# Weight loading with separate result tiles, three landing buffers and shifts shared between two engines

## Chip, core and metric

The kernel runs on one core of one Trainium2 chip. The metric is the device time of one execution in microseconds (us); the kernel before was timed three times, and the median of those runs is the figure to compare with. One further execution was taken with the hardware profiler, and all rows of the profile below come from that one.

## The reference

The inputs are q, k and v of shape 8 x 8 x 576 x 64 (batch, heads, sequence, head size) and two weight matrices, `w_in` (512 x 2048) and `w_out` (2048 x 512), all float32 in meaning. The weights reach the kernel as 64-bit words, so each weight takes 8 bytes in memory.

```python
scores = q @ k.T / sqrt(64)
# heads 0..3: keys 0 <= query - key < 32; heads 4..7: key <= query, key % 32 == query % 32
attn   = softmax(where(mask, scores, -1e9))
x      = (attn @ v)            # regrouped to 4608 tokens x 512
h      = x @ w_in
out    = (h * cos(h)) @ w_out  # 4608 x 512, float32
```

## The kernel before

**Blocks and chunks.** The feed-forward part runs over 12 blocks `j` of 384 tokens, and in each over 16 chunks `f` of 128 hidden features. `hidden(j, f)` (L353 to L376) makes 12 matmuls into one of two PSUM banks named `h`: every product of float32 numbers is made of three products of a high and a low half (`wi_h`, `wi_l`, `x_hi`, `x_lo`). Then ScalarE rounds h / 2 pi (L364), VectorE reduces the argument (L365), ScalarE takes the sine (L368), VectorE multiplies with h (L371), ScalarE makes the high half `g_hi` (L374) and GpSimd the low half `g_lo` (L375). The bank is free again when L371 has read it. `outer(j, f)` adds nine matmuls (L382) with `wo_h` and `wo_l`; it runs three chunks behind `hidden` (`LAG = 3`).

**Stages.** First comes the attention of batches 0 and 1, with matmuls that only keep TensorE busy (L442). In it `load_x` (L341 to L352) brings blocks 0 and 1 from `xT`, a buffer in device memory to which attention writes its results. The second stage alternates chunks of blocks 0 and 1 while the weights arrive: the loop calls `need_weights(f)`, `chunk(0, f)`, `need_weights(f + 2)` and `chunk(1, f - 1)`. At its end it loads block 2. The third stage interleaves blocks 2 to 11 with the attention of batches 2 to 7.

**A weight load.** `load_weight` (L111 to L130) is called 32 times, for `w_in` and `w_out` of each of the 16 chunks. It takes one tile `raw` of 128 x 512 pairs of 32-bit words (512 KB) from the pool `cv`, which has two buffers, and fills it by one DMA from the queue of SyncE, SP (L114). The pairs are the low and the top words of float64 numbers. Five passes put the float32 together inside `raw` itself and split it: VectorE shifts the low words right by 29 (L116), VectorE adds the sign (L119), ScalarE scales the top words (L124), VectorE shifts and merges them in (L125), ScalarE makes the high half (L129), GpSimd subtracts to get the low half (L130). L130 reads the tile as well, so the buffer can be filled again only after L130.

**Order.** The program is laid out by a planner that simulates its time and puts each engine's instructions in one fixed order; on the chip every engine and every DMA queue runs its own list in that order, and an instruction that waits holds up all behind it. `order` adds an edge for the planner: L116 of chunk `f` comes no earlier than the VectorE step L365 of chunk `f - 2` of block 0. From block 2 on, `in_turn` fixes the order of the matmuls.

**x.** `load_x` lands each of the four 128 x 384 tiles of a block in a tile `x_raw` from its own pool with two buffers (L347); VectorE copies it to `x_hi` (L348) and GpSimd writes the difference to `x_lo` (L349). `x_hi` and `x_lo` have eight buffers each, so two blocks.

Of the kernel before, what the change touches and what calls it, by code (L numbers as in the profile page):

```python
# [12 lines left out]
F32 = mybir.dt.float32  # L13
F32R = mybir.dt.float32r
BF16 = mybir.dt.bfloat16
I32 = mybir.dt.int32
AF = mybir.ActivationFunctionType
ALU = mybir.AluOpType
AX = mybir.AxisListType
# [5 lines left out]
P = 128  # L25
# [18 lines left out]
TB = 384  # L44
# [24 lines left out]
def attention_cos_ffn(ctx, tc, qkl, vl, qkvs, w_in, w_out, eye, eye16, mask_l0, mask_l, mask_s, out):  # L69
    nc = tc.nc  # L70

    const = ctx.enter_context(tc.tile_pool(name="const", bufs=1))
# [1 line left out]
    ps_h = ctx.enter_context(tc.tile_pool(name="ps_h", bufs=2, space=bass.MemoryType.PSUM))  # L74
    ps_o = ctx.enter_context(tc.tile_pool(name="ps_o", bufs=1, space=bass.MemoryType.PSUM, reuse_waits="tile"))
    sm = ctx.enter_context(tc.tile_pool(name="sm", bufs=4))
    xp = ctx.enter_context(tc.tile_pool(name="xp", bufs=2))
    rp = ctx.enter_context(tc.tile_pool(name="rp", bufs=2))
    xs = ctx.enter_context(tc.tile_pool(name="xs", bufs=2 * NKC))

# [4 lines left out]
    ms = const.tile([P, GB], BF16, name="ms")  # L85
    for t, src in ((ident16, eye16), (ms, mask_s), (ident, eye), (ml0, mask_l0), (ml, mask_l)):
        nc.scalar.dma_start(out=t, in_=src)
    shift1, shift2, quarter = (const.tile([P, 1], F32, name=n) for n in ("shift1", "shift2", "quarter"))
    for t, value in ((shift1, -SHIFT), (shift2, -SHIFT - STEP), (quarter, math.pi / 2.0)):
        nc.vector.memset(t, value)  # L90
    warm = const.tile([P, 64], BF16, name="warm")
# [7 lines left out]
    def order(later, first, reason):  # L99
        tc.add_manual_dep(  # L100
            later.ins, first.ins.name,
            mybir.DependencyInfo(mybir.DependencyClass.NoSync, mybir.DependencyReason.DATA), reason=reason,
        )

    wi_h = const.tile([P, NFC, NKC, P], F32R, name="wi_h")
    wi_l = const.tile([P, NFC, NKC, P], F32R, name="wi_l")
    wo_h = const.tile([P, NFC, DM], F32R, name="wo_h")
    wo_l = const.tile([P, NFC, DM], F32R, name="wo_l")
    xT = dram.tile([P, NKC, NTOK], F32, name="xT")

    def load_weight(cv, src, hi, lo, after):  # L111

        raw = cv.tile([P, 512, 2], I32, name="raw")
        nc.sync.dma_start(out=raw.rearrange("p n w -> p (n w)"), in_=src)  # L114
        low, top = raw[:, :, 0], raw[:, :, 1]
        first = nc.vector.tensor_scalar(out=low, in0=low, scalar1=29, scalar2=None, op0=ALU.logical_shift_right)  # L116
        if after is not None:
            order(first, after, "weights no earlier than they are needed")
        nc.vector.scalar_tensor_tensor(  # L119
            out=low, in0=top, scalar=-0x80000000, in1=low, op0=ALU.bitwise_and, op1=ALU.bitwise_or  # L120
        )


        nc.scalar.activation(out=top.bitcast(F32), in_=top.bitcast(F32), func=AF.Copy, scale=2.0 ** -112)  # L124
        nc.vector.scalar_tensor_tensor(  # L125
            out=low, in0=top, scalar=3, in1=low, op0=ALU.logical_shift_left, op1=ALU.bitwise_or
        )
        w = low.bitcast(F32)
        nc.scalar.copy(out=hi, in_=w)  # L129
        nc.gpsimd.tensor_tensor(out=lo, in0=w, in1=hi.bitcast(F32), op=ALU.subtract)  # L130

    weights = 0

    def need_weights(cv, f):
        nonlocal weights
        for f in range(weights, f + 1):
            after = reduced[f - AHEAD] if 0 <= f - AHEAD < len(reduced) else None
            load_weight(
                cv, w_in.bitcast(I32)[f], wi_h[:, f].rearrange("p c n -> p (c n)"),
                wi_l[:, f].rearrange("p c n -> p (c n)"), after,  # L140
            )
            load_weight(cv, w_out.bitcast(I32)[f], wo_h[:, f], wo_l[:, f], after)
            weights = f + 1

    turn = None
# [9 lines left out]
    class Attention:  # L155
# [39 lines left out]
        def softmax(self, s, mask, n, w, pn=None):  # L195
# [15 lines left out]
            if self.plain:  # L211
                exps.append(nc.scalar.activation(out=e, in_=t, func=AF.Exp, scale=0.125))
            else:
                nc.scalar.activation(out=e, in_=t, func=AF.Silu, bias=shift1, scale=0.0625)  # L214
                nc.scalar.activation(out=t, in_=t, func=AF.Silu, bias=shift2, scale=0.0625)
                nc.vector.scalar_tensor_tensor(
                    out=e, in0=t, scalar=-math.exp(STEP), in1=e, op0=ALU.mult, op1=ALU.add
                )
                nc.scalar.activation(out=e, in_=e, func=AF.Square, scale=math.exp(SHIFT) / STEP)
            z = sm.tile([P, SU], F32, name="z")  # L220
# [120 lines left out]
    def load_x(j):  # L341
        his, los = [], []
        for c in range(NKC):
            raw = xp.tile([P, TB], F32, name="x_raw")
            hi = xs.tile([P, TB], F32R, name="x_hi")
            lo = xs.tile([P, TB], F32R, name="x_lo")
            nc.sync.dma_start(out=raw, in_=xT[:, c, j * TB:(j + 1) * TB])  # L347
            nc.vector.tensor_copy(out=hi, in_=raw)  # L348
            nc.gpsimd.tensor_tensor(out=lo, in0=raw, in1=hi.bitcast(F32), op=ALU.subtract)  # L349
            his.append(hi)  # L350
            los.append(lo)
        return his, los  # L352

    def hidden(j, f, x_hi, x_lo):
# [7 lines left out]
        r = rp.tile([P, TB], F32, name="r")  # L362
        k = r.bitcast(I32)
        nc.scalar.activation(out=k, in_=h, func=AF.Copy, scale=1.0 / (2.0 * math.pi), bias=0.25)  # L364
        red = nc.vector.scalar_tensor_tensor(out=r, in0=k, scalar=-2.0 * math.pi, in1=h, op0=ALU.mult, op1=ALU.add)  # L365
# [31 lines left out]
    def chunk(j, f, x, acc):  # L397
        pend.append((j, f, *hidden(j, f, *x), acc))
        if len(pend) > LAG:
            outer(*pend.pop(0))  # L400

    def accumulators(pool):
        return [pool.tile([P, DM], F32, name=f"acc{t}") for t in range(NTT)]

    def in_stages(units, knots, lag):


        begun = np.interp(range(len(units)), [n for _, n in knots], [at for at, _ in knots]).astype(int).tolist()
        steps = {}
        for n, (at, unit) in enumerate(zip(begun, units)):  # L410
            second = min([at + lag] + begun[n + 2:n + 3])
            for stage in (at, second, second + 1):
                steps.setdefault(stage, []).append(unit)
        return steps
# [9 lines left out]
    def step(steps, n):  # L424
        for unit in steps.get(n, ()):
            next(unit, None)

    with ExitStack() as loading:
        cv = loading.enter_context(tc.tile_pool(name="cv", bufs=2))
        with ExitStack() as stack:  # L430

            ps = stack.enter_context(tc.tile_pool(name="ps", bufs=1, space=bass.MemoryType.PSUM, reuse_waits="tile"))
            att = Attention(
                stack, True, ((ps_h, "h"), (ps_h, "h"), (ps, "acc0")), ((ps_o, "acc0"), (ps_o, "acc1")),
                ((ps_o, "acc2"), (ps, "acc3")), ld_bufs=3,
            )
            steps = in_stages(att.units(0) + att.units(1), ((0, 0), (20, 20)), 2)
            spare = ps.tile([P, 512], F32, name="acc2")

            def keep_busy(n, after):  # L440
                for _ in range(n):
                    mm = nc.tensor.matmul(  # L442
                        spare[:64], warm, warm.unsqueeze(1).broadcast_to([P, 8, 64]), start=True, stop=True
                    )
                    if after is not None:
                        order(mm, after, "in its place")
                    after = mm

            keep_busy(BUSY[0], None)
            for n in range(max(steps) + 1):  # L450
                step(steps, n)
                if n + 1 < len(BUSY):
                    keep_busy(BUSY[n + 1], att.scored)
                if n == LOADS[0]:
                    x0 = load_x(0)
                if n == LOADS[1]:
                    x1 = load_x(1)

        gp = ctx.enter_context(tc.tile_pool(name="gp", bufs=LAG + 1, side="right", reuse_waits="tile"))

        with ExitStack() as stack:
            op = stack.enter_context(tc.tile_pool(name="op", bufs=2, reuse_waits="tile"))
            ps_o1 = stack.enter_context(
                tc.tile_pool(name="ps_o1", bufs=1, space=bass.MemoryType.PSUM, reuse_waits="tile")
            )
            acc0, acc1 = accumulators(ps_o), accumulators(ps_o1)
            for f in range(NFC + 1):
                if f < NFC:
                    need_weights(cv, f)
                    chunk(0, f, x0, acc0)  # L470
                    need_weights(cv, min(f + AHEAD, NFC - 1))
                if f >= 1:
                    chunk(1, f - 1, x1, acc1)
            cur, acc = load_x(2), accumulators(ps_o)
            for f in range(LAG):
                chunk(2, f, cur, acc)


    with ExitStack() as stack:
# [6 lines left out]
        for n in range(LAG, (NTB - 2) * NFC):  # L486
            j, f = 2 + n // NFC, n % NFC
# [105 lines left out]
```

## Time and profile before

| what | value |
|---|---|
| runs | 1000.22, 1000.85, 1001.1 us; median 1000.85 |
| profiled execution | 999.46 us, of which the span of the core 997.7 us |
| mean granted TensorE clock | 0.995 |
| TensorE busy with matmuls | 968.3 us, 97% of the span |
| VectorE, ScalarE, GpSimd busy | 466.5, 499.2 and 385.2 us |
| bytes moved by DMA | 80.14 MB, of which 32 weight loads of 512 KB |

In the profile PE is TensorE, PEld its weight loads, DVE VectorE, ACT ScalarE, POOL GpSimd and SP SyncE; a q behind a name is the engine's DMA or instruction queue. A row of groups gives line, engine, operation, output and input tiles, the count, then busy time in us and the mean of one in ns, then the idle time before it and what ended it. A row of waits reads "who waited <- for what: us in total, times, longest us". A row of windows gives, for a stretch of the span, the busy time of each engine with its number of instructions, then the granted TensorE clock, the share of the DMA engines in use, and GB/s.

### The profile page before, as it was taken

To read this page: it belongs to the slowest core of one execution; us is meant where nothing else is said; L and a number is where in the kernel's file an instruction comes from. 1 tells how busy PE (TensorE), PEld (TensorE's weight loads), DVE (VectorE), ACT (ScalarE), POOL (GpSimd) and SP (SyncE) were. 2 spreads that over 40 slices of the span, in tenths; PEclk is the share of its full clock that TensorE was granted. 3 is DMA by queue.
4 is the path that set the end of the run, shared out by engine and by line. 5 is a ranking of instruction groups with operands and counts; after the bars stand their busy time and mean duration, and the time that the engine had idled before them with its cause. 6 is when DMAs were issued, how large, how long until landed. Compare 5 with 4: busy or idle time off the path is not lost.

```text
span 997.7 us, 17749 instructions
## 1 busy us (share of the span) xinstructions
PE 968.3 (97%) x6890; PEld 847.5 (85%) x6890; DVE 466.5 (47%) x1005; ACT 499.2 (50%) x1043; POOL 385.2 (39%) x418
## 2 busy tenths in 40 slices
PE   8988988998999999999999999999999999999998
PEld 5777877877888888888888888888888888889997
DVE  6866677655454444434344444444344444322222
ACT  3655555565555555455445545554454544433433
POOL 2555554544344344333333344434243333332221
PEclk9999999999899999999999999999999999999999
DMA  8963333232322222111211322211221310100000
GB/s 247 300 199 103 111 108 112 80 105 73 102 85 88 70 79 84 42 50 59 83 58 35 110 79 76 82 50 53 88 59 34 98 55 29 41 20 1 33 1 32
DMA packets 48228, 80.14 MB, mean 80 GB/s; under 512 B 5904, under 2 KB 33296, under 8 KB 48144
## 3 DMA queue, kind: packets, MB, share of 16 engines
q1 hardware_dynamic: 38208, 69.35, 23.1%
q10 hardware_dynamic: 9936, 9.65, 2.8%
q8 instruction: 54, 0.88, 0.4%
q14 instruction: 30, 0.25, 0.1%
HBM read 60.11 MB, written 18.87 MB: 79 GB/s over the span
## 4 chain that ended last, share of the span: by engine, by line
PE 78%; DMA 4%; DVE 2%; ACT 1%; issue 1%; POOL 0%; DVEq 0%; POOLq 0%; ACTq 0%; SPq 0%
PE h L358 35%; PE acc L382 34%; DMA raw<-in_w_out 2%; PE acc L249 2%; PE acc L265 2%; PE acc L316 2%; PE acc L290 2%; PE acc L257 1%; PE acc L302 1%; DVE raw L116 1%; DMA raw<-in_w_in 1%; DMA xT<-x_t 0%; ACT r L368 0%; DVE r L371 0%; DVE raw L119 0%
## 5 line engine op out<-in xcount | busy, mean ns | idle before, releaser
L375 POOL TENSOR_TENSOR g_lo<-r,g_hi 128x384 fp32r<-128x384 f32 x192 | 198.3, 1033 | 396.6 <-issue 249.2
L358 PE MATMUL h<-x_hi,wi_h 128*128 128x384 f32 x768 | 267.9, 349 | 13.7 <-DVE r L371 13.7
L358 PE MATMUL h<-x_hi,wi_l 128*128 128x384 f32 x768 | 259.7, 338 | 0.0
L358 PE MATMUL h<-x_lo,wi_h 128*128 128x384 f32 x768 | 259.4, 338 | 0.0
L365 DVE SCALAR_TENSOR_TENSOR r<-r,h 128x384 f32<-128x384 int32 x192 | 106.1, 552 | 270.8 <-ACT r L364 247.7
L382 PE MATMUL acc<-wo_l,g_hi 128*128 128x512 f32 x576 | 227.4, 395 | 0.0
L382 PE MATMUL acc<-wo_h,g_hi 128*128 128x512 f32 x576 | 224.2, 389 | 1.4 <-ACT g_hi L374 1.4
L382 PE MATMUL acc<-wo_h,g_lo 128*128 128x512 f32 x576 | 224.6, 396 | 0.0
L358 PEld LDWEIGHTS h<-x_hi,wi_h 128*128 128x128 f32 x768 | 145.2, 189 | 31.0 <-DVE r L371 19.8
L368 ACT ACTIVATE r<-r,quarter 128x384 f32<-128x384 f32 x192 | 118.5, 617 | 96.5 <-DVE r L365 96.2
L358 PEld LDWEIGHTS h<-x_lo,wi_h 128*128 128x128 f32 x768 | 145.3, 189 | 5.0
L371 DVE TENSOR_TENSOR r<-r,h 128x384 f32<-128x384 f32 x192 | 106.0, 552 | 84.0 <-ACT r L368 83.4
L358 PEld LDWEIGHTS h<-x_hi,wi_l 128*128 128x128 f32 x768 | 145.1, 189 | 0.1
L364 ACT ACTIVATE r<-h 128x384 int32<-128x384 f32 x192 | 93.4, 487 | 102.0 <-PE h L358 95.5
L374 ACT CAST g_hi<-r 128x384 fp32r<-128x384 f32 x192 | 98.3, 512 | 87.5 <-DVE r L371 87.2
L382 PEld LDWEIGHTS acc<-wo_h,g_lo 128*128 128x128 f32 x576 | 108.0, 188 | 22.8
L382 PEld LDWEIGHTS acc<-wo_h,g_hi 128*128 128x128 f32 x576 | 108.3, 188 | 19.0 <-ACT g_hi L374 1.7
L382 PEld LDWEIGHTS acc<-wo_l,g_hi 128*128 128x128 f32 x576 | 108.0, 187 | 18.2
L349 POOL TENSOR_TENSOR x_lo<-x_raw,x_hi 128x384 fp32r<-128x384 f32 x48 | 50.9, 1062 | 130.9 <-DVE x_hi L348 107.4
L214 ACT ACTIVATE e_sb<-t_sb,shift 128x288 f32<-128x288 f32 (+1 forms) x60 | 32.9, 548 | 95.6 <-POOL t_sb L206 95.6
L348 DVE CAST x_hi<-x_raw 128x384 fp32r<-128x384 f32 x48 | 21.6, 452 | 60.9 <-DMA x_raw<-xT 60.2
L206 POOL TENSOR_TENSOR t_sb<-t_sb,mx 128x288 f32<-128x288 f32 (+1 forms) x60 | 41.6, 693 | 16.9 <-DVE mx L205 11.5
(66 smaller groups left out, 855.8 us busy)
## 6 DMA issues: line engine op xcount, KB each, us to landing
qk<-in_qkvs SPq DMA_DIRECT2D x32, 324.0 KB, 3.7
qk<-in_qkl SPq DMA_DIRECT2D x48, 208.0 KB, 3.3
x_raw<-xT SPq DMA_DIRECT2D x48, 192.0 KB, 2.4
out<-o SPq DMA_DIRECT2D x36, 256.0 KB, 2.1
raw<-in_w_in SPq DMA_DIRECT2D x16, 512.0 KB, 3.7
raw<-in_w_out SPq DMA_DIRECT2D x16, 512.0 KB, 3.8
v<-in_vl SPq DMA_DIRECT2D x48, 144.0 KB, 2.2
xT<-x_t ACTq DMA_DIRECT2D x16, 288.0 KB, 3.5
```

Of the source, the lines that this page charges most:

```text
L206: nc.gpsimd.tensor_tensor(out=t, in0=t, in1=mx[:, :n].unsqueeze(2).broadcast_to([P, n, w]), op=ALU.subtract)
L214: nc.scalar.activation(out=e, in_=t, func=AF.Silu, bias=shift1, scale=0.0625)
L348: nc.vector.tensor_copy(out=hi, in_=raw)
L349: nc.gpsimd.tensor_tensor(out=lo, in0=raw, in1=hi.bitcast(F32), op=ALU.subtract)
L358: mm = nc.tensor.matmul(h, w[:, f, c], x[c], start=(i == 0), stop=(i == len(ops) - 1))
L364: nc.scalar.activation(out=k, in_=h, func=AF.Copy, scale=1.0 / (2.0 * math.pi), bias=0.25)
L365: red = nc.vector.scalar_tensor_tensor(out=r, in0=k, scalar=-2.0 * math.pi, in1=h, op0=ALU.mult, op1=ALU.add)
L368: sin = nc.scalar.activation(out=r, in_=r, func=AF.Sin, bias=quarter)
L371: nc.vector.tensor_tensor(out=r, in0=r, in1=h, op=ALU.mult)
L374: nc.scalar.copy(out=g_hi, in_=r)
L375: nc.gpsimd.tensor_tensor(out=g_lo, in0=r, in1=g_hi.bitcast(F32), op=ALU.subtract)
L382: mm = nc.tensor.matmul(acc[t], g[:, ts], w[:, f], start=(f == 0 and i == 0), stop=(f == NFC - 1 and i == 2))
```

## The change

The kernel after differs in three places. In `load_weight` the float32 is put together in a tile of its own, `bits` (128 x 512, two buffers), and `raw` has three buffers; what reads `raw` last is then L125 of the kernel before. For `w_out` the first shift is done by a ScalarE activation that reads the low word as an unsigned integer, multiplies, adds a bias and rounds to an integer; for `w_in` it stays on VectorE. The ordering edge is kept for the VectorE shift only. In `load_x` the DMA lands in the tile of the low half, and GpSimd subtracts in place; the pool of `x_raw` is gone. Three small constants share one tile.

```diff
-    xp = ctx.enter_context(tc.tile_pool(name="xp", bufs=2))
...
-    shift1, shift2, quarter = (const.tile([P, 1], F32, name=n) for n in ("shift1", "shift2", "quarter"))
+    biases = const.tile([P, 3], F32, name="biases")
+    shift1, shift2, quarter = (biases[:, n:n + 1] for n in range(3))
...
-    def load_weight(cv, src, hi, lo, after):
+    def load_weight(cv, src, hi, lo, after, scalar):
...
-        first = nc.vector.tensor_scalar(out=low, in0=low, scalar1=29, scalar2=None, op0=ALU.logical_shift_right)
-        if after is not None:
-            order(first, after, "weights no earlier than they are needed")
+        bits, scaled = cv.tile([P, 512], I32, name="bits", bufs=2), top.bitcast(F32)
+        if scalar:
+            nc.scalar.activation(
+                out=bits, in_=low.bitcast(U32), func=AF.Copy, scale=2.0 ** -29 * (1.0 - 2.0 ** -16),
+                bias=7.5 * 2.0 ** -16 - 0.5,
+            )
+        else:
+            first = nc.vector.tensor_scalar(out=bits, in0=low, scalar1=29, scalar2=None, op0=ALU.logical_shift_right)
+            if after is not None:
+                order(first, after, "weights no earlier than they are needed")
         nc.vector.scalar_tensor_tensor(
-            out=low, in0=top, scalar=-0x80000000, in1=low, op0=ALU.bitwise_and, op1=ALU.bitwise_or
+            out=bits, in0=top, scalar=-0x80000000, in1=bits, op0=ALU.bitwise_and, op1=ALU.bitwise_or
         )
...
         nc.vector.scalar_tensor_tensor(
-            out=low, in0=top, scalar=3, in1=low, op0=ALU.logical_shift_left, op1=ALU.bitwise_or
+            out=bits, in0=top, scalar=3, in1=bits, op0=ALU.logical_shift_left, op1=ALU.bitwise_or
         )
-        w = low.bitcast(F32)
+        w = bits.bitcast(F32)
...
-                wi_l[:, f].rearrange("p c n -> p (c n)"), after,
+                wi_l[:, f].rearrange("p c n -> p (c n)"), after, False,
...
-            load_weight(cv, w_out.bitcast(I32)[f], wo_h[:, f], wo_l[:, f], after)
+            load_weight(cv, w_out.bitcast(I32)[f], wo_h[:, f], wo_l[:, f], after, True)
...
-            raw = xp.tile([P, TB], F32, name="x_raw")
             hi = xs.tile([P, TB], F32R, name="x_hi")
             lo = xs.tile([P, TB], F32R, name="x_lo")
+            raw = lo.bitcast(F32)
...
-        cv = loading.enter_context(tc.tile_pool(name="cv", bufs=2))
+        cv = loading.enter_context(tc.tile_pool(name="cv", bufs=3))
```

More of the change, by code (lines that the diff above doesn't have):

```diff
@@ L16 @@
 I32 = mybir.dt.int32
+U32 = mybir.dt.uint32
 AF = mybir.ActivationFunctionType
@@ L115, in load_weight @@
         low, top = raw[:, :, 0], raw[:, :, 1]
-        first = nc.vector.tensor_scalar(out=low, in0=low, scalar1=29, scalar2=None, op0=ALU.logical_shift_right)
-        if after is not None:
-            order(first, after, "weights no earlier than they are needed")
+        bits, scaled = cv.tile([P, 512], I32, name="bits", bufs=2), top.bitcast(F32)
[8 more added lines that the diff above has]
+                order(first, after, "weights no earlier than they are needed")
         nc.vector.scalar_tensor_tensor(
-            out=low, in0=top, scalar=-0x80000000, in1=low, op0=ALU.bitwise_and, op1=ALU.bitwise_or
+            out=bits, in0=top, scalar=-0x80000000, in1=bits, op0=ALU.bitwise_and, op1=ALU.bitwise_or
         )
-        nc.scalar.activation(out=top.bitcast(F32), in_=top.bitcast(F32), func=AF.Copy, scale=2.0 ** -112)
+        nc.scalar.activation(out=scaled, in_=scaled, func=AF.Copy, scale=2.0 ** -112)
         nc.vector.scalar_tensor_tensor(
-            out=low, in0=top, scalar=3, in1=low, op0=ALU.logical_shift_left, op1=ALU.bitwise_or
+            out=bits, in0=top, scalar=3, in1=bits, op0=ALU.logical_shift_left, op1=ALU.bitwise_or
         )
-        w = low.bitcast(F32)
+        w = bits.bitcast(F32)
         nc.scalar.copy(out=hi, in_=w)
```

## The prediction

> **What bounds the kernel now.** I read the page first, then the stretches of the span, then who waits in the stretch where TensorE is not full.
>
> ```profile
> span 997.7 us, 17749 instructions
> PE 968.3 (97%) x6890; PEld 847.5 (85%) x6890; DVE 466.5 (47%) x1005; ACT 499.2 (50%) x1043; POOL 385.2 (39%) x418
> ```
>
> ```profile
> 0.00:50.00 50.00, 46.25 (x674) 30.95 (x674) 37.08 (x112) 25.37 (x62) 21.45 (x31) 1.00 0.87 273
> 50.00:75.00 25.00, 20.91 (x171) 17.93 (x167) 15.54 (x31) 13.84 (x30) 13.02 (x12) 1.00 0.64 199
> 75.00:206.00 131.00, 119.41 (x576) 103.82 (x575) 87.73 (x133) 71.82 (x134) 69.06 (x57) 0.99 0.31 100
> 206.00:251.00 45.00, 38.77 (x366) 33.80 (x365) 23.17 (x53) 27.18 (x58) 17.50 (x21) 0.97 0.29 91
> 251.00:850.00 599.00, 599.00 (x4368) 532.20 (x4369) 264.23 (x608) 303.37 (x654) 227.69 (x261) 1.00 0.23 69
> ```
>
> TensorE sets the end: from 251 to 850 us it has no idle time at all, so nothing that the change does to later blocks can shorten or, unless it adds a wait there, lengthen the run. What can be won lies ahead of that: 131.00 - 119.41 = 11.6 us idle in the streaming of the weights (75 to 206), 4.1 us in 50 to 75 and 6.2 us in 206 to 251. The next rows are the waits of TensorE and VectorE in the streaming stage, and those of SP's queue.
>
> ```profile
> PE h L358 <- DVE r L371: 11.6, 11, 3.0
> DVE raw L116 <- DMA raw<-in_w_out: 9.5, 11, 1.4
> DVE raw L116 <- DMA raw<-in_w_in: 4.2, 5, 2.0
> SPq L114 <- POOL wi_l L130: 60.3, 12, 7.0
> SPq L114 <- POOL wo_l L130: 43.7, 12, 4.9
> ```
>
> All of TensorE's idle time there is one wait: `hidden` has no free bank because VectorE has not done L371. VectorE in turn stands 13.7 us at L116, a shift whose weights have not landed, and L371 and L365 are queued behind that. The weights are late because their DMA may be issued only when GpSimd has done L130 on the tile that lay in the buffer. The chain of waits shows one turn of the `w_out` buffer, with the two passes the chain leaves out added from the timeline:
>
> ```profile
> 139.29 3.75 DMA raw<-in_w_out
> 143.13 1.01 DVE raw L116
> 144.16 0.70 DVE raw L119
> 144.93 0.44 ACT raw L124
> 146.39 0.64 ACT wo_h L129
> 148.51 3.73 DMA raw<-in_w_out
> ```
>
> ```profile
> 145.63 0.69 DVE L125 SCALAR_TENSOR_TENSOR raw<-raw 128x512 int32<-128x512 int32 x1 [0.32 <-ACT raw L124]
> 147.16 1.32 POOL L130 TENSOR_TENSOR wo_l<-raw,wo_h 128x512 fp32r<-128x512 f32 x1
> ```
>
> From issue to issue this is 148.51 - 139.29 = 9.22 us, and nearly all of it is work in series: landing, five passes, GpSimd. TensorE's own need is less:
>
> ```profile
> 195.45 2.08 PE acc L382 x9
> 197.53 2.10 PE h L358 x12
> ```
>
> Two chunks per `f` take 2 x (2.10 + 2.08) = 8.36 us. So with two buffers the turn of the buffer is 0.86 us longer than TensorE's work: the landing buffers pace this stage, not an engine (VectorE, the busiest helper, has 87.73 of 131 us).
>
> **The change part by part.**
>
> *Third buffer, freed at L125.* A landing tile is now held for 3.75 of landing and then up to the end of L125, which in the rows above is 146.32 - 139.29 = 7.0 us, and there are three for two loads per 8.36 us: a tile may be held 12.5 us before it paces TensorE. The new tile `bits` is held from the shift to the end of L130, 148.48 - 143.13 = 5.4 us, and two of them allow 8.36. Both leave over 2 us for queueing, so the 13.7 us of L116 waiting for DMA should go, and with them most of TensorE's 11.6. To these I add the clock: after a wait of 3.00 us the matmuls ran slow,
>
> ```profile
> 87.94 0.69 PE L358 MATMUL h<-x_hi,wi_h 128*128 128x384 f32 x1 [3.00 <-DVE r L371]
> ```
>
> and the stretch's mean clock of 0.99 is 1.3 us over 131. The most there is to win is 11.6 + 1.3 = 12.9 us. The least is 0, if something else in the same fixed lists becomes late. I take 80%, 10.3 us, because the passes still meet each other on VectorE. The Trainium skill ("TensorE: Matmul & The Clock Gate", Part 1) puts the clock's drop behind an idle window of about 3.4 us; no stall in this stage is that long and the clock fell at 3.00, so here the row and not the rule's length counts. By the rule as stated the 1.3 us would not hang on these stalls, and the sum would be 1.0 us smaller.
>
> *The `w_out` shift on ScalarE.* It removes 16 of 32 shifts from VectorE and adds 16 activations of 128 x 512 words to ScalarE.
>
> ```profile
> L116 DVE TENSOR_SCALAR raw<-raw 128x512 int32<-128x512 int32 x32 | 22.7, 712 | 20.9 <-DMA raw<-in_w_out 11.6 <-DMA raw<-in_w_in 9.0 <-POOL g_lo L375 0.2
> L116 DVE TENSOR_SCALAR raw<-raw x32: 387/542/1582, 12.4 to 190.4; 128x512 int32<-128x512 int32 x32
> L124 ACT ACTIVATE raw<-raw 128x512 f32<-128x512 f32 x32 | 21.6, 673 | 29.6 <-DVE raw L119 27.7 <-POOL wi_l L130 1.5
> L364 ACT ACTIVATE r<-h 128x384 int32<-128x384 f32 x192 | 93.4, 487 | 102.0 <-PE h L358 95.5 <-POOL g_lo L375 5.9
> ```
>
> VectorE gives up 16 x 0.712 = 11.4 us (between 16 x 0.387 = 6.2 and 16 x 1.582 = 25.3). The new activation isn't in this trace; the nearest rows are L124, the same shape and stride (0.673), and below it L364, smaller but with an integer result (0.487). I take 0.67: 10.8 us, bounds 7.8 to 16 (at 1 us each, for an integer input that costs more). Over the streaming stage, 14 of the 16, ScalarE goes from 71.8 to 81.2 us in about 119, 68%, and VectorE from 87.7 to 77.7, 65%. Neither is a bound, so I cost the move itself at nothing on the path; its cover is the slack of the two `h` banks. A bank is filled at the end of one `hidden` and wanted again after the next `hidden` and two `outer`s, 2.10 + 2 x 2.08 = 6.3 us. The chain that frees it takes 0.49 (L364) and three more:
>
> ```profile
> L365 DVE SCALAR_TENSOR_TENSOR r<-r,h 128x384 f32<-128x384 int32 x192 | 106.1, 552 | 270.8 <-ACT r L364 247.7 <-POOL e_sb L225 17.6 <-ACT t_sb L215 2.3
> L368 ACT ACTIVATE r<-r,quarter 128x384 f32<-128x384 f32 x192 | 118.5, 617 | 96.5 <-DVE r L365 96.2
> L371 DVE TENSOR_TENSOR r<-r,h 128x384 f32<-128x384 f32 x192 | 106.0, 552 | 84.0 <-ACT r L368 83.4
> ```
>
> 0.49 + 0.55 + 0.62 + 0.55 = 2.2 us, so 4.1 us are left for waiting. Without that cover the move costs the 10.8. The Trainium skill ("ScalarE: Activation LUTs", Rules for kernel authors) speaks against this part: plain arithmetic belongs on VectorE, and ScalarE is to be budgeted at about 0.3 us plus 0.83 ns per element. That makes an estimate of 0.72 us for this pass by the page, against 0.673 in the row; the sum is the same by either as long as the slack holds.
>
> *An earlier third load.* The first stage has the DMA engines at 0.87 and 273 GB/s, and TensorE already waits there for its inputs:
>
> ```profile
> PE h L249 <- DMA qk<-in_qkl: 1.5, 2, 1.3
> ```
>
> One more 512 KB transfer is drawn in there; at 273 GB/s it takes 1.9 us from the transfers beside it. Bounds 0 and 1.9; I take 0.9 lost.
>
> *50 to 75 us.* Of the 4.1 us idle, 2.1 is the same wait for L371:
>
> ```profile
> PE h L358 <- DVE r L371: 2.1, 1, 2.1
> 59.95 0.36 DVE L348 CAST x_hi<-x_raw 128x384 fp32r<-128x384 f32 x1 [1.43 <-DMA x_raw<-xT]
> 61.43 0.44 PE L358 MATMUL h<-x_hi,wi_h 128*128 128x384 f32 x1 [2.13 <-DVE r L371]
> ```
>
> L371 stood behind two shifts, a sign pass and a copy that waited 1.43 us for x. One shift goes and the x transfers no longer wait for `x_raw`; bounds 0 and 2.1, I take 1.0 won.
>
> *x into the low half's tile.* Copies and subtractions keep their number. What moves is the start of the four DMAs of block 2: their target is now freed by the last matmul of `hidden(0, 15)`, whereas two were landed long before.
>
> ```profile
> 193.10 2.35 PE h L358 x12
> 198.23 2.27 SPq L347 DMA_DIRECT2D x_raw<-xT  x2
> 203.78 1.02 POOL L349 TENSOR_TENSOR x_lo<-x_raw,x_hi 128x384 fp32r<-128x384 f32 x1 [0.29 <-DVE x_hi L348]
> 205.97 2.10 PE h L358 x12
> ```
>
> ```profile
> x_raw<-xT SPq DMA_DIRECT2D x48, 192.0 KB, 2.4
> ```
>
> `hidden(0, 15)` ends at 195.45 and block 2 starts 10.5 us later. In that time go 2.4 us of landing (the page's median), one copy and four subtractions of 1.02 with two of `g_lo` between them, 2.4 + 0.4 + 6 x 1.02 = 8.9 us. That fits by 1.6 us. Queued behind these DMAs on SP are only output stores and the third stage's loads, wanted later. Price 0; bounds -1 to +3.
>
> *Sum.* -10.3 - 1.0 + 0.9 = -10.4 us against the profiled execution, 999.46 (span 997.7 and 1.8 around it), gives 989.1. The median of the runs stands 1.39 above the profiled one, so I forecast 990.5.
>
> **The rivals.**
>
> *VectorE's fixed list keeps half of the stalls.* If L371 is late because of L119, L125 and GpSimd beside them rather than because of the landing, only the clearest DMA waits go. For it: the median of L116 is 0.542 but its longest 1.582, so passes are stretched beyond what a landing explains. Against it: VectorE is at 67% there. It gives about half of the 10.4: 995.5 (994.9 to 998.8).
>
> The Trainium skill ("SBUF — State Buffer", two separate sides) says a VectorE pass with two SBUF inputs and a GpSimd pass lock each other out. The spread of L116 agrees, and L119 and L125 remain such passes.
>
> *It doesn't do what it says.* If the planner puts the third load behind passes that end as late as L130, SP issues as now: 1000.9, within 0.2% (about 2 us, what a measurement of this kernel can tell from no change). Against it: SP waits for L130 itself in 104 us of rows above, and that edge is gone.
>
> *Slower: ScalarE waits in VectorE's place.* The `w_out` shift stands on ScalarE in front of L364 and L368, and the landing it waits for was 9.5 of the 13.7 us. If `w_out` still lands late, ScalarE takes these waits over, the bank is freed as late as now, and 14 passes of 0.67 us come on top: 1000.85 + 9.4 = 1010. It decides from where a ScalarE wait plus the pass exceeds the 4.1 us of slack. Against it: the landing should now come over 2 us ahead.
>
> *More than forecast.* All of the 12.9 and 2.1 and some of the 6.2 us after 206 give 17 or more: 983 or below.
>
> **How the numbers follow.** Forecast (gain of 6 to 15 us, 985.9 to 994.8) 0.56; half of it 0.17; no change 0.09; slower 0.13; more than forecast 0.05. The likeliest gives 990.5. The range 982 to 1000 takes in the half case, the edge of no change and most of the larger gain, and leaves the slower case out. Faster 0.56 + 0.17 + 0.05 = 0.78, same 0.09, slower 0.13.
>
> **What would show it.** Right: in 75 to 206 TensorE's idle time falls under 3 us; VectorE no longer waits for `raw` landings; SP's waits in that stage name L125 and sum to no less than now, since loads run ahead; the stage ends near 195. Right for ScalarE: its shift near 0.67 us, with no wait for a landing ahead of it. Wrong: TensorE's waits for L371 stay above 6 us, or move to `x_lo` at the start of block 2, or to `qk` in the first 50 us; or the clock falls below 0.99 after a new stall of 3 us.

## The result, and the profile after

The kernel after takes 990.28 us (median of six runs, 987.89 to 994.36); the kernel before, in the same comparison, 999.21 us (six runs, 996.1 to 1001.1). The ratio is 0.9923, with a 95% interval of 0.9903 to 0.9943, which is 7.7 us; the two medians lie 8.9 us apart. The profiled execution of after took 991.56 us. In what follows its lines are: L116 the DMA of a weight, L121 the shift on ScalarE, L126 the shift on VectorE, L129 the sign, L134 the scaling, L135 the merge, L139 and L140 the two halves; `load_x` is L357 to L359, `hidden` L368 to L385, `outer` L392. L371 of before is L381.

The page of after, and then its stretches with the same bounds as before:

```profile
span 989.8 us, 17730 instructions
PE 972.3 (98%) x6890; PEld 850.7 (86%) x6890; DVE 445.4 (45%) x989; ACT 507.9 (51%) x1059; POOL 385.7 (39%) x418
```

```profile
0.00:50.00 50.00, 45.87 (x659) 30.99 (x660) 37.56 (x104) 24.49 (x60) 22.01 (x30) 0.97 0.86 283
50.00:75.00 25.00, 21.67 (x163) 17.63 (x158) 17.12 (x35) 15.87 (x35) 13.71 (x13) 0.80 0.56 172
75.00:206.00 131.00, 131.00 (x676) 117.79 (x674) 72.72 (x130) 85.86 (x160) 72.01 (x62) 1.00 0.32 112
206.00:251.00 45.00, 38.70 (x357) 33.85 (x354) 22.83 (x58) 24.02 (x52) 16.81 (x22) 0.92 0.31 88
251.00:850.00 599.00, 599.00 (x4357) 529.54 (x4356) 258.31 (x597) 303.42 (x652) 227.71 (x260) 1.00 0.22 67
```

The streaming stage (75 to 206) is full: 131.00 of 131 us, where it had 11.6 us idle. Yet the run won less than that. The page says why: the span is TensorE's busy plus its idle time. Before, that was 968.3 + 29.4; after, 972.3 + 17.5. Idle time fell by 11.9 us, and the same 6890 matmuls took 4.0 us longer. So two questions go into the experiments: which part of the change emptied the idle time, and what made the matmuls slower.

The waits in the streaming stage, of SP's queue in after:

```profile
SPq L116 <- DVE bits L135: 54.3, 20, 5.1
SPq L116 <- DMA raw<-in_w_out: 23.5, 9, 2.9
```

SP now waits for VectorE's merge, and for 23.5 us for landings, where it waited for GpSimd's L130. No shift waits for a landing in this stage. The longest of TensorE's waits over the whole run:

```profile
PE acc L267 <- POOL e_sb L235: 4.2, 2, 3.2
PE h L368 <- DVE r L381: 2.3, 1, 2.3
PE acc L312 <- POOL pn_s L235: 2.2, 1, 2.2
PE h L259 <- DMA qk<-in_qkl: 1.4, 1, 1.4
```

One wait for the product is left of twelve, and it lies outside the stage. The timeline around it, VectorE first, then TensorE:

```profile
58.92 0.72 DVE L126 TENSOR_SCALAR bits<-raw 128x512 int32<-128x512 int32 x1
60.15 0.36 DVE L358 CAST x_hi<-x_lo 128x384 fp32r<-128x384 f32 x1 [0.52 <-DMA x_lo<-xT]
60.43 2.10 DVE L129 SCALAR_TENSOR_TENSOR bits<-raw,bits 128x512 int32<-128x512 int32 x2
62.45 0.54 DVE L381 TENSOR_TENSOR r<-r,h 128x384 f32<-128x384 f32 x1
```

```profile
60.21 0.53 PE L267 MATMUL acc<-ident,e_sb 128*96 128x128 f32 x3 [0.96 <-POOL e_sb L235]
63.04 0.69 PE L368 MATMUL h<-x_hi,wi_h 128*128 128x384 f32 x1 [2.30 <-DVE r L381]
63.53 0.52 PE L368 MATMUL h<-x_lo,wi_h 128*128 128x384 f32 x1
63.85 0.52 PE L368 MATMUL h<-x_hi,wi_l 128*128 128x384 f32 x1
```

The product (L381) is queued behind two sign passes of 2.10 us together. TensorE stands 0.96 us, works 0.53, stands 2.30, and then its matmuls start 0.32 us apart instead of the 2.10 / 12 = 0.175 us that they take elsewhere. The stretch of 60 to 70 us, in after and then in before:

```profile
60.00:70.00 10.00, 7.49 (x41) 5.79 (x41) 7.75 (x11) 5.37 (x13) 5.45 (x5) 0.60 0.44 142
```

```profile
60.00:70.00 10.00, 7.16 (x45) 6.17 (x46) 5.87 (x11) 4.72 (x10) 7.69 (x6) 1.00 0.59 154
```

The clock granted is 0.60 against 1.00, and 0.89 in the ten us that follow. In short stretches of 0.2 us it is 0.50 from 62.0 to 72.2 us, so it fell while TensorE still stood. At half the pace, the matmuls from 63.04 on lose about half of these 9.2 us, 4.6 by this estimate. It is not the only such stretch: after is at half clock from 24.4, 62.0, 215.6 and 239.5 us on, for 20.5 us in all, and before from 87.4 and 247.9 us on, for 10.2 us. That is 10.2 us of full pace lost in after against 5.1 in before, in step with the mean granted clock of the two profiled executions, 0.990 and 0.995.

### The profile page after: what moved, and what is told of

It reads as the page before. It is cut to its first block, busy times and chain, and to the rows that moved or that the text cites. A ratio compares the mean times of both kernels' runs of the same rounds, so it can differ in the third digit from the quotient of the medians.

```text
span 989.8 us, 17730 instructions
## 1 busy us (share of the span) xinstructions
PE 972.3 (98%) x6890; PEld 850.7 (86%) x6890; DVE 445.4 (45%) x989; ACT 507.9 (51%) x1059; POOL 385.7 (39%) x418
## 4 chain that ended last, share of the span: by engine, by line
PE 93%; DMA 4%; DVE 1%; ACT 1%; POOL 0%; issue 0%; SPq 0%; POOLq 0%; ACTq 0%
PE h L368 41%; PE acc L392 40%; PE acc L275 2%; PE acc L259 2%; PE acc L326 2%; PE acc L300 2%; PE acc L267 1%; PE acc L312 1%; DMA x_lo<-xT 1%; DMA xT<-x_l 1%; DMA raw<-in_w_out 1%; PE acc L452 1%; DMA qk<-in_qkl 1%; DMA xT<-x_t 0%; PE h L300 0%
## 5 line engine op out<-in xcount | busy, mean ns | idle before, releaser
L385 POOL TENSOR_TENSOR g_lo<-r,g_hi 128x384 fp32r<-128x384 f32 x192 | 199.2, 1038 | 416.5 <-issue 264.4
L368 PE MATMUL h<-x_hi,wi_h 128*128 128x384 f32 x768 | 267.2, 348 | 2.3 <-DVE r L381 2.3
L368 PE MATMUL h<-x_hi,wi_l 128*128 128x384 f32 x768 | 260.8, 340 | 0.0
L368 PE MATMUL h<-x_lo,wi_h 128*128 128x384 f32 x768 | 259.5, 338 | 0.0
L392 PE MATMUL acc<-wo_h,g_hi 128*128 128x512 f32 x576 | 227.7, 395 | 0.0
L392 PE MATMUL acc<-wo_l,g_hi 128*128 128x512 f32 x576 | 227.4, 395 | 0.0
L392 PE MATMUL acc<-wo_h,g_lo 128*128 128x512 f32 x576 | 226.1, 395 | 0.0
L378 ACT ACTIVATE r<-r,biases 128x384 f32<-128x384 f32 x192 | 118.5, 617 | 85.1 <-DVE r L375 83.0
L368 PEld LDWEIGHTS h<-x_hi,wi_h 128*128 128x128 f32 x768 | 145.6, 190 | 14.5 <-DVE r L381 2.5
L368 PEld LDWEIGHTS h<-x_lo,wi_h 128*128 128x128 f32 x768 | 145.9, 190 | 6.1
L368 PEld LDWEIGHTS h<-x_hi,wi_l 128*128 128x128 f32 x768 | 145.4, 189 | 0.2
L381 DVE TENSOR_TENSOR r<-r,h 128x384 f32<-128x384 f32 x192 | 106.0, 552 | 83.5 <-ACT r L378 83.1
L392 PEld LDWEIGHTS acc<-wo_h,g_lo 128*128 128x128 f32 x576 | 107.7, 187 | 26.2
L392 PEld LDWEIGHTS acc<-wo_h,g_hi 128*128 128x128 f32 x576 | 108.1, 188 | 18.5 <-ACT g_hi L384 0.4
L392 PEld LDWEIGHTS acc<-wo_l,g_hi 128*128 128x128 f32 x576 | 108.3, 188 | 18.1
L359 POOL TENSOR_TENSOR x_lo<-x_lo,x_hi 128x384 fp32r<-128x384 f32 x48 | 50.8, 1058 | 127.5 <-DVE x_hi L358 106.0
L224 ACT ACTIVATE e_sb<-t_sb,biases 128x288 f32<-128x288 f32 (+1 forms) x60 | 32.9, 549 | 102.8 <-POOL t_sb L216 102.8
L358 DVE CAST x_hi<-x_lo 128x384 fp32r<-128x384 f32 x48 | 21.0, 439 | 69.6 <-DMA x_lo<-xT 69.5
```

Of the source, the lines that this page charges most:

```text
L368: mm = nc.tensor.matmul(h, w[:, f, c], x[c], start=(i == 0), stop=(i == len(ops) - 1))
L378: sin = nc.scalar.activation(out=r, in_=r, func=AF.Sin, bias=quarter)
L381: nc.vector.tensor_tensor(out=r, in0=r, in1=h, op=ALU.mult)
L385: nc.gpsimd.tensor_tensor(out=g_lo, in0=r, in1=g_hi.bitcast(F32), op=ALU.subtract)
L392: mm = nc.tensor.matmul(acc[t], g[:, ts], w[:, f], start=(f == 0 and i == 0), stop=(f == NFC - 1 and i == 2))
```

## The experiments

The table gives each run by its edit, its ratio to the kernel before with the interval, and TensorE's busy and idle time from the page of its profiled execution (idle is span less busy). The last column is the steady time of a chunk, one `hidden` and one `outer`, from the chain of waits between 900 and 970 us.

| run | ratio to before | busy, us | idle, us | a chunk, us |
|---|---|---|---|---|
| before | 1 | 968.3 | 29.4 | 4.187 |
| after | 0.9923 [0.9903, 0.9943] | 972.3 | 17.5 | 4.200 |
| 1 third buffer alone | 0.9976 [0.9958, 0.9995] | 965.8 | 26.2 | 4.187 |
| 2 own tiles alone | 0.9889 [0.9869, 0.991] | 967.6 | 18.5 | 4.187 |
| 3 shift on ScalarE alone | 0.9951 [0.993, 0.9971] | 968.4 | 20.8 | 4.187 |
| 4 after with two buffers | 0.9934 [0.9912, 0.9957] | 971.9 | 22.1 | 4.200 |
| 5 own tiles and ScalarE shift | 0.991 [0.9882, 0.9937] | 966.2 | 20.8 | 4.187 |
| 6 x in the low half alone | 1.0015 [0.9999, 1.0032] | 970.4 | 28.6 | 4.187 |
| 7 constants in one tile alone | 1.0032 [1.0014, 1.0049] | 974.6 | 25.3 | 4.200 |
| 8 after, all shifts on VectorE | 0.9934 [0.9903, 0.9964] | 973.3 | 20.9 | 4.200 |
| 9 after, constants apart again | 0.9797 [0.9778, 0.9817] | 959.8 | 18.1 | 4.127 |
| 10 run 9, edge at the product | 0.9764 [0.9741, 0.9788] | 958.7 | 17.9 | 4.127 |
| 11 run 2, edge at the product | 0.9897 [0.988, 0.9915] | 968.2 | 17.8 | 4.187 |
| 12 run 7 with 64 bytes of padding | one execution, 995.9 us | 967.9 | 26.2 | 4.160 |

Where the expectations use letters, A is the theory that the landing buffers and their release pace the streaming stage, B in runs 1 and 3 the rival that VectorE's load does, and C the rival that ScalarE takes over VectorE's waits.

**Run 1, the third buffer alone,** on the kernel before:

```diff
-        cv = loading.enter_context(tc.tile_pool(name="cv", bufs=2))
+        cv = loading.enter_context(tc.tile_pool(name="cv", bufs=3))
```

> The kernel before with three landing buffers and nothing else. Theory A (the landing buffers pace the streaming stage): the turn of a buffer, 9.2 us, is now shared by three for two loads, 12.5 us of TensorE work, so the 11.6 us of TensorE waiting in 75 to 206 us fall below 3 and the time falls by 6 to 10 us against the kernel before. Rival B (VectorE's load is what counts, and its shifts must move): idle stays above 8 us and the time within 2 us of before.

The gain is a quarter of a per cent, and the stalls of TensorE, 6.9 us, lie between the two bounds that were set (under 3 and over 8), so neither theory is met as stated. The waits of the streaming stage (75 to 195 us), first of SP's queue, then of VectorE and TensorE:

```profile
SPq L114 <- POOL wi_l L130: 76.1, 11, 7.9
SPq L114 <- POOL wo_l L130: 16.5, 11, 4.8
```

```profile
DVE raw L116 <- DMA raw<-in_w_out: 13.7, 11, 1.6
PE h L358 <- DVE r L371: 6.9, 10, 0.9
```

The DMA still waits for GpSimd's L130, up to 7.9 us at a time, and VectorE still stands 13.7 us at landings. The timeline shows how long a tile is held, from its issue to the end of L130:

```profile
138.46 0.33 SPq L114 DMA_DIRECT2D raw<-in_w_in  x1
154.36 1.31 POOL L130 TENSOR_TENSOR wi_l<-raw,wi_h 128x512 fp32r<-128x512 f32 x1
```

That is 17.2 us for this `w_in` tile, and its shift comes only at 147.71. The `w_out` tiles beside it are held 10.5 us. The mean, 13.9 us, is above the 12.5 us that three buffers allow. A buffer more doesn't help much while each is held to the last pass of its chain.

**Run 2, the own tiles alone:** two landing buffers, every shift on VectorE, but the float32 put together in `bits`, so that `raw` is free after VectorE's merge.

```diff
-        first = nc.vector.tensor_scalar(out=low, in0=low, scalar1=29, scalar2=None, op0=ALU.logical_shift_right)
+        bits = cv.tile([P, 512], I32, name="bits", bufs=2)
+        first = nc.vector.tensor_scalar(out=bits, in0=low, scalar1=29, scalar2=None, op0=ALU.logical_shift_right)
...
-        w = low.bitcast(F32)
+        w = bits.bitcast(F32)
```

> The kernel before with the float32 put together in its own tile, two landing buffers, all shifts on VectorE, x as before. A buffer is now held for 7.0 us and two allow 8.36. Theory A: most of the stall goes, 4 to 9 us faster than before, with 1 to 5 us of TensorE idle left in the stage because 1.4 us of slack is little. Rival B: within 2 us of before.

The same waits, of VectorE and TensorE, and then of SP's queue:

```profile
DVE bits L117 <- DMA raw<-in_w_out: 2.7, 2, 1.6
PE h L359 <- DVE r L372: 2.1, 1, 2.1
```

```profile
SPq L114 <- DVE bits L126: 56.5, 23, 6.2
SPq L114 <- DMA raw<-in_w_in: 22.9, 9, 3.0
```

This part alone takes 10.9 us out of TensorE's idle time and makes the kernel 1.1% faster, at least as much as the whole change does (the intervals just overlap). Landing buffers are as many as before; what changed is which engine lets one go (`bits` adds two tiles of half the size).

**Run 3, the `w_out` shift on ScalarE alone,** in place in `raw`, on the kernel before:

```diff
+        if scalar:
+            nc.scalar.activation(
+                out=low, in_=low.bitcast(U32), func=AF.Copy, scale=2.0 ** -29 * (1.0 - 2.0 ** -16),
+                bias=7.5 * 2.0 ** -16 - 0.5,
+            )
```

> The kernel before with only the w_out shift moved to ScalarE, inside raw, two landing buffers. Theory A: the turn of a buffer keeps its length (a pass of 0.66 in place of one of 0.71), so the time stays within 2 us of before. Rival B: VectorE loses 11 us of passes and the time falls by 4 us or more. Rival C (ScalarE takes over the wait for the landing): slower by 2 to 9 us, with a ScalarE wait for raw in front of the chain that frees the banks.

It is neither without effect nor slower: 0.9951, 6.5 us by the medians. That meets the bound set for rival B, VectorE's load (4 us or more). Its waits in the stage:

```profile
DVE raw L123 <- DMA raw<-in_w_in: 17.1, 11, 2.0
PE h L365 <- DVE r L378: 4.6, 10, 0.7
ACT raw L118 <- DMA raw<-in_w_out: 1.0, 3, 0.6
```

ScalarE takes over 1.0 us of landing waits, not the 9.5 that VectorE had, so the slower rival falls. VectorE waits longer for landings than before (17.1 against 13.7 us), all of them now for `w_in`, and yet TensorE's wait for the product fell from 11.6 to 4.6 us. The sum of VectorE's landing waits is therefore not what TensorE pays. That VectorE has 8.0 us less work in 75 to 206 us (79.7 against 87.7) would fit, and so would one place per chunk where it waits, instead of two; no run separates them.

**Run 4, after with two landing buffers,** and **run 8, after with every shift on VectorE:**

```diff
-        cv = loading.enter_context(tc.tile_pool(name="cv", bufs=3))
+        cv = loading.enter_context(tc.tile_pool(name="cv", bufs=2))
```

> The kernel after with two landing buffers in place of three. Theory A: 7.0 us of hold against 8.36 still nearly fits; TensorE's idle time in the stage is 0 to 4 us and the time lies within 3 us of the kernel after. If instead the third buffer is what counts, idle comes back to 6 us or more and the time is within 3 us of the kernel before. The first 50 us tell about the third load that is drawn into them: the first hidden matmul starts near 50 us as in before, not near 52.7 as in after.

```diff
-            load_weight(cv, w_out.bitcast(I32)[f], wo_h[:, f], wo_l[:, f], after, True)
+            load_weight(cv, w_out.bitcast(I32)[f], wo_h[:, f], wo_l[:, f], after, False)
```

> The kernel after with all 32 shifts on VectorE. If the own tiles and the third buffer do the work, idle time in 75 to 206 us stays below 2.5 us and the time within 3 us of the kernel after; if the move to ScalarE is needed for a full TensorE, idle is 4 us or more and the time 3 to 8 us longer than the kernel after.

Both give 0.9934, inside the interval of after. In the streaming stage TensorE is idle for 0.9 us in run 4 and 0.6 in run 8. Once the tiles are apart, neither the third buffer nor the ScalarE shift can be told from nothing. Run 4 also tests the price that the prediction put on the third load, since it has none:

```profile
PE h L259 <- DMA qk<-in_qkl: 3.9, 2, 3.5
PE acc L259 <- DMA qk<-in_qkl: 2.0, 2, 1.7
```

These are waits of its first 75 us. With two buffers TensorE waits longer for `qk` than with three (1.4 and 0.4 us in after), and its first `hidden` starts at 57.7 us against 52.8 in after and 50.1 in before. The own tiles alone (run 2) start at 52.4. So the later start doesn't need the third load.

**Run 5, the parts of runs 2 and 3 together, with two buffers:**

> The kernel before with the float32 in its own tiles and the w_out shift on ScalarE, two landing buffers, x and the constants as before. The first four runs gave 0.989 for the own tiles alone. If the two parts add, TensorE's idle time in 75 to 206 us goes to 0 to 1 us and the time is 0.985 to 0.989 of the kernel before; if ScalarE's shift only covers what the own tiles already cover, it is the same as the own tiles alone within 2 us. Nine outer matmuls should take 2.08 us as in the kernel before.

0.991, not better than run 2 alone, with 2.4 us idle in the streaming stage (run 2: 1.7). The two gains don't add: both take from the same idle time.

**Run 6, x landing in the low half's tile alone:**

```diff
-            raw = xp.tile([P, TB], F32, name="x_raw")
...
+            raw = lo.bitcast(F32)
```

> The kernel before with x landing in the low half's tile and nothing else. My theory: no effect on the streaming stage, time within 2 us of before; the first hidden matmul, 50.1 us in before, stays within 1.5 us. Rival D (the x part is what delays the first stage of the kernel after, where it starts at 52.8, and of the one with two buffers, 57.7): it starts 2 us or more later and the time is 1 to 4 us longer. If the x tiles are what makes nine outer matmuls take 2.10 us in place of 2.08, it shows here.

No effect that can be told (1.0015, interval 0.9999 to 1.0032); the first hidden matmul starts at 51.3 us, within the bound, and nine outer matmuls take 2.08.

**Run 7, the three constants in one tile alone.** This small edit changes no instruction's work. But each tile of one column takes 32 bytes of a partition, so that all that is allocated behind it, the weights, x and the rest, starts 64 bytes lower, as it does in after.

```diff
-    shift1, shift2, quarter = (const.tile([P, 1], F32, name=n) for n in ("shift1", "shift2", "quarter"))
+    biases = const.tile([P, 3], F32, name="biases")
+    shift1, shift2, quarter = (biases[:, n:n + 1] for n in range(3))
```

> The kernel before with the three constants in one tile, which shifts the places of the weights in SBUF and changes nothing else. If the places are what makes nine outer matmuls take 2.10 us in place of 2.08, it shows here, as 192 times 0.013 = 2.6 us more over the span; if not, the time is within 1 us of before.

It is slower, 1.0032 with an interval that leaves out 1, and it has the steady pace of after. Two pieces of its chain of waits (start, duration, what), far from any stall:

```profile
905.91 2.10 PE h L359 x12
908.01 2.10 PE acc L383 x9
```

Before has 2.10 and 2.08 there. As a mean over many chunks, one takes 4.200 against 4.187 us, and 192 chunks make that 2.5 us.

**Run 9, after with the constants apart again,** and one buffer fewer in a small pool of the softmax, since 32 bytes were wanting otherwise:

```diff
-    biases = const.tile([P, 3], F32, name="biases")
-    shift1, shift2, quarter = (biases[:, n:n + 1] for n in range(3))
+    shift1, shift2, quarter = (const.tile([P, 1], F32, name=n) for n in ("shift1", "shift2", "quarter"))
...
-            mx = sm.tile([P, SU], F32, name="mx")
+            mx = sm.tile([P, SU], F32, name="mx", bufs=3)
```

> The kernel after with the three constants in tiles of their own again, so that the weights lie where they lie in the kernel before (32 bytes for it come from three instead of four buffers for mx). If the places of the weights cost what the run with the constants alone showed, nine outer matmuls take 2.08 us again and the time is 2 to 3 us below that of the kernel after, 0.989 to 0.990 of the kernel before.

The expectation missed: the pace doesn't go back to that of before, it falls well below it, and the kernel takes 979.36 us (0.9797). Its page, and two pieces of its chain:

```profile
span 977.9 us, 17733 instructions
PE 959.8 (98%) x6890; PEld 848.5 (87%) x6890; DVE 447.6 (46%) x989; ACT 506.6 (52%) x1059; POOL 385.5 (39%) x418
```

```profile
906.14 2.08 PE h L367 x12
908.22 2.04 PE acc L391 x9
```

The idle time is that of after within 0.6 us; all of the difference, 12.5 us, is in the busy time of the same number of matmuls. The groups of `outer` between 251 and 850 us, where TensorE never stands and the clock is 1.00 in each, in before, after and run 9 (count, then busy us and mean ns of one):

```profile
L382 PE MATMUL acc<-wo_l,g_hi 128*128 128x512 f32 x362 | 143.0, 395 | 0.0
L382 PE MATMUL acc<-wo_h,g_lo 128*128 128x512 f32 x361 | 142.8, 396 | 0.0
L382 PE MATMUL acc<-wo_h,g_hi 128*128 128x512 f32 x362 | 140.7, 389 | 0.0
```

```profile
L392 PE MATMUL acc<-wo_h,g_lo 128*128 128x512 f32 x362 | 142.7, 394 | 0.0
L392 PE MATMUL acc<-wo_l,g_hi 128*128 128x512 f32 x362 | 142.6, 394 | 0.0
L392 PE MATMUL acc<-wo_h,g_hi 128*128 128x512 f32 x362 | 142.6, 394 | 0.0
```

```profile
L391 PE MATMUL acc<-wo_h,g_hi 128*128 128x512 f32 x369 | 143.8, 390 | 0.0
L391 PE MATMUL acc<-wo_h,g_lo 128*128 128x512 f32 x368 | 143.3, 389 | 0.0
L391 PE MATMUL acc<-wo_l,g_hi 128*128 128x512 f32 x368 | 143.2, 389 | 0.0
```

One product of the three is fast in before (389 ns against 395), none in after (394), and all three in run 9 (389 and 390): 369 of them fit in where 362 did.

**Run 12, run 7 with 64 bytes of padding** between the tiles of `w_in` and those of `w_out`: `w_in` lies lower than before, and all that is behind it where it was.

```diff
+    pad = const.tile([P, 16], F32, name="pad")
+    nc.vector.memset(pad, 0.0)
```

> The kernel before with the constants in one tile and 64 unused bytes between the tiles of w_in and w_out: w_in lies 64 bytes lower than before, w_out and everything after it where it lay. If the place of w_out (or of what lies behind it) makes nine outer matmuls take 2.10 us, they take 2.08 here; if the place of w_in or the shared tile of the constants does, 2.10.

```profile
909.38 2.08 PE h L361 x12
911.46 2.08 PE acc L385 x9
```

Nine outer matmuls are back at 2.08 us, as was expected if the place of `w_out`, or of what lies behind it, sets them. Twelve hidden ones, which take 2.10 in before and in run 7, take 2.08 too, and that was not expected. It makes a third pace, 4.160 us a chunk, so it is not the merged tile of constants that made run 7 slow: this kernel has it too, and differs by padding alone (and one fill of it). Where the tiles start sets how fast the matmuls go: in the table, kernels with the same places have the same pace, whatever else differs between them. Which tile against which isn't settled. Modulo 128 bytes, `w_in`, `w_out` and the x tiles start at 96, 96 and 96 in before and runs 1 to 3, 5, 6 and 11, at 32, 32 and 32 in after and runs 4, 7 and 8, at 32, 96 and 96 in run 12, and at 96, 96 and 64 in runs 9 and 10. The hidden matmuls, which read `w_in` and x, take 2.10 us where these two agree and 2.08 to 2.09 where they differ (runs 9, 10 and 12); that is a pattern, not a test. For the outer ones the two tiles that a matmul reads can't be all: `wo_h`, `wo_l`, `g_hi` and `g_lo` lie at the same addresses in before and in run 9, as the kernels are built, and nine matmuls take 2.08 us there and 2.04 here. Whether it is TensorE's reads that meet, or its reads with those of other engines, was not tried.

**Runs 10 and 11, the ordering edge moved** from the reduction (L365 of before) to the product (L371), in run 9's kernel and in run 2's:

```diff
-        if j == 0:
-            reduced.append(red)
...
-        nc.vector.tensor_tensor(out=r, in0=r, in1=h, op=ALU.mult)
+        prod = nc.vector.tensor_tensor(out=r, in0=r, in1=h, op=ALU.mult)
+        if j == 0:
+            reduced.append(prod)
```

> The run before it, with the planner's edge moved: the first VectorE shift of chunk f comes after L371 (the product that frees a bank of h) of chunk f - 2 of block 0, not already after L365. In the kernel after, L371 of the first chunk stands behind 2.8 us of weight passes, TensorE idles 2.3 us at 63 us and runs at a lower clock until 72. If that stall goes, 2 us of it and up to 4 us of clock go with it, 0.983 to 0.987 of the kernel before; if the planner only puts the same passes elsewhere on the way, the same as the run before it.

> The kernel before with the float32 in its own tiles (two landing buffers, all shifts on VectorE, x and constants as before) and the planner's edge moved as in the run before it. The own tiles alone gave 0.989; the same stall before the first product was 0.9 us there and another of 2.1 at 77 us. If it goes, 0.985 to 0.988; else 0.989.

Run 10 is the fastest kernel of this study, 976.01 us, 0.9764 of before; its expected range was counted from what run 9 was to be, and missed with it. Its stall for the product is short, by its timeline:

```profile
65.75 0.44 PE L367 MATMUL h<-x_hi,wi_h 128*128 128x384 f32 x1 [0.51 <-DVE r L378]
```

0.51 us instead of 2.30. But its interval and that of run 9 overlap (0.9741 to 0.9788 against 0.9778 to 0.9817), and on run 2's kernel the edge brought nothing (0.9897 against 0.9889). In its trace the clock is at half from 66.6 to 70.0 us all the same. So the shorter stall is seen, and a gain from it isn't shown.

## Why the prediction was right, and where it was not

The forecast, 990.5 us, lies 0.2 us from the median. Part of that is luck: the sum gave 10.4 us off the profiled execution, which lost 7.9 (999.46 to 991.56); and the median of before that it was set beside, 1000.85, came out at 999.21 with more runs. The executions of after themselves lie between 987.89 us (mean granted clock 0.995) and 994.36 (0.986).

**The bound.** Right. The landing buffers paced the streaming stage, and the product stood behind a shift that waited for its weights. What the landings cost is looser than the prediction had it, which let VectorE's 13.7 us of waits and TensorE's 11.6 go together: in run 1 they are 13.7 and 6.9 us, in run 3 17.1 and 4.6. With the waits gone, TensorE's idle time there is 0; block 2 starts at 194.85 us instead of 205.97, where the prediction said near 195. One sign of it missed: SP's waits for the weights' loads sum to 77.8 us in the rows above, against 104.0 before, and were to be no less.

**"Third buffer, freed at L125", 10.3 us.** Undersized: it took 80%, and all 11.6 us came. It also held two edits for one. By its arithmetic of turns a third buffer would have done without an earlier release: three tiles held 9.22 us each against 12.5 allowed. Run 1 refutes that (6.9 us of stalls left), run 2 shows that the release is what counts, and run 4 that the third buffer isn't needed. The one turn that it took as its measure, of a `w_out` tile with two buffers, left out that a tile landed early stands until VectorE and then GpSimd reach it in their own fixed lists: in run 1 the `w_in` tiles are held 17.2 us, and SP waits up to 7.9 us at a time for L130.

**The shift on ScalarE, at nothing.** Right for this change:

```profile
L121 ACT ACTIVATE bits<-raw x16: 652/656/681, 13.4 to 168.0; 128x512 int32<-128x512 uint32 x16
```

0.656 us against 0.67 taken, no wait for a landing in the stage, and run 8 can do without it. The row of the Trainium skill that the prediction quotes ("ScalarE: Activation LUTs", Rules for kernel authors) gives its 0.3 us for a bias passed as a pointer operand. In this pass scale and bias are constants, and the estimate of 0.72 us by that row lies above what was measured. But the reason, that the move is off the path, holds only once the tiles are apart. On the kernel before it takes 8.6 us of idle time (run 3).

**"An earlier third load", 0.9 us lost.** Not borne out. TensorE is idle 0.4 us longer in the first 50 us (4.13 against 3.75), but run 4, without the third load, starts later still. The edits give the planner another order of the first stage, with `qk` loads at other places; which edit moves the start isn't settled.

**"50 to 75 us", 1.0 won.** Wrong in sign once the clock is counted. TensorE's idle time there fell from 4.1 to 3.3 us, but the wait for the product, which was to shrink, is 2.30 us where it was 2.13: behind the copy of x stand two sign passes instead of one. And the clock fell within it, which costs about 4.6 us. The prediction named a fall of the clock only after a stall of 3 us, as what would prove it wrong; here stalls of 0.96 and 2.30 us with 0.53 us of work between them were enough. The Trainium skill ("TensorE: Matmul & The Clock Gate", Part 1) has the clock at half or full, set by windows of about 3.4 us that run freely. The trace agrees: start-to-start times of 0.32 against 0.175 us, a granted clock of 0.50, and half-clock stretches of after that begin 11.0, 45.0 and 7.0 times 3.41 us apart. The Trainium skill asks for an idle window there; here one with 2.2 us of idle time, from 58.6 to 62.0, sufficed. In before the stall of 2.13 us lay across two such windows, with 1.4 and 1.3 us idle, and the clock stayed at 1.00. So whether a stall of this size costs the clock is in part luck, in the forecast and in the run.

**x, at nothing.** Right. The row of the last low half, and that of TensorE's first matmuls of block 2 from the chain of waits, leave slack:

```profile
188.17 2.04 POOL L359 TENSOR_TENSOR x_lo<-x_lo,x_hi 128x384 fp32r<-128x384 f32 x2 [0.30 <-DVE x_hi L358]
```

```profile
194.85 2.10 PE h L368 x12
```

The low half ends at 190.2, and block 2 starts at 194.85 with no idle time before it; run 6 shows no effect.

**The step that was missing.** Three constants in one tile had no price in the prediction, and it said that nothing in 251 to 850 us could change unless a wait is added there. No wait was added, and the pace of the matmuls changed all the same. By run 7 that costs 2.5 us of steady pace (3.2 us by the ratio). The half clock, which had no term for new falls either, took about 5 us more than in before (10.2 against 5.1). Together these are more than the 4.0 us of busy time that the sum lacked; what made up for the rest isn't separated.

**The slower rival** fell with run 3, **half of the stalls** and **no change** with the empty streaming stage.

## What to carry to other kernels

Ask of a landing buffer which instruction reads it last and on whose fixed list that stands; a small tile of one's own that lets the buffer go after the first engines can be worth more than another buffer. Keep span, busy and idle time of the bounding engine apart: here idle time fell as forecast, and busy time, taken as fixed, rose. After any edit of the allocations, compare the mean of one matmul in a stretch without waits, since a few bytes of shift can undo a good part of a gain or double it. And before a term of a few us is read out of one profile, see how many stretches at half clock each profile has.

## What the runs showed of the hardware

Where tiles start within SBUF moved the pace of float32 matmuls, at the same granted clock, from 4.127 to 4.200 us for the same 21 matmuls: 0.073 x 192 = 14 us of this kernel, more than the change itself brought. Shifts of 32 and 64 bytes did it. The Trainium skill ("SBUF — State Buffer", Operand start alignment) allows any start that is a multiple of the element size and says that its runs timed nothing; no run here contradicts that, and these are times for it.

The granted clock keeps to steps. In each of the fourteen traces the first 960 us can be cut into steps of 3.41 us so that the clock is 1.00 or 0.50 throughout each step; a step at half loses 1.7 us of full pace. Before has three steps at half, after six, run 1 only one. In these traces the clock fell 47 times, each time behind a step with 1.2 us or more of TensorE's idle time, and each step at full clock with more than 1.9 us idle was followed by one at half; in between both occur. So what counts is how much of a stall lies in one step. The same wait for `pn_s` shows it: 2.23 us, ending at 225.49, left the clock of before at 1.00, with 1.5 us of it in one step; 2.21 us, ending at 214.37, cost after a step at half.
